# The first feed-forward product on four row strips of the array instead of one full pass

## The chip, the cores and the metric

The kernel runs on one core of one Trainium2 chip. A core has a matrix engine (TensorE, PE in the profile, with its weight loads listed as PEld), a vector engine (DVE), a scalar engine (ACT), GpSimd (POOL) and a queue that issues DMAs (SP). The metric is the device time of one launch in microseconds (us). Before the change the median is 1633.15 us, of two runs at 1631.74 and 1634.57.

## The reference

An induced-attention layer over four batches of 12480 rows with 128 channels, then a feed-forward layer with squared ReLU and 2048 units, all in float32:

```python
def mab(q, kv):
    s = scale * (q @ kv.transpose(0, 2, 1))
    s = s - s.max(-1, keepdims=True)
    a = np.exp(s)
    a /= a.sum(-1, keepdims=True) + 1e-09
    return a @ kv
h = mab(I, x)                       # 32 inducing rows attend to x
attn = mab(x, h)                    # x attends to the 32 rows
y = np.maximum(attn @ w_in, 0.0)
out = y * y @ w_out
```

The second attention gives `attn = a @ h` with only 32 weights a row, so `attn @ w_in = a @ (h @ w_in)`: the kernel forms `h @ w_in` (32 rows x 2048 units) once a batch, and the first feed-forward product contracts over 32 rows, not over 128 channels.

## The kernel before, in words

**Units.** Each batch is cut into 13 units of 960 rows, a unit into two blocks of 480 rows. For each unit `First` does the attention of the 32 inducing rows (scores, exponentials, a mix into a running sum). When a batch is through, `first_end` closes it: it makes `hT` (channels x 32 rows) and then `hw`, the product `h @ w_in`, in four tiles `hw0` to `hw3` of 512 units each (`wide`, `part`, `rest` inside it, lines 612 to 627). `Second` does the other attention for a unit: its scores go into a narrow PSUM tile `na`, and nine DVE steps and one ACT step (`weigh`) turn them into weights `sw`, which are written to DRAM (`far`, line 716) and read back in another layout (`st`, line 721).

**Precision.** Products that matter run in the type float32r, whose operands are rounded. Each value is therefore split in a rounded part ("hi") and the rest ("lo"). In `hw` before the change, rows 0 to 63 hold the hi part and rows 64 to 127 the lo part; in `st` the 128 rows hold hi and lo of the 32 weights twice. So a single product over 128 rows adds up all four combinations, hi and lo of `hw` with hi and lo of `st`. `pairs` (line 232) spreads the 32 columns of `hT` over 128 places for that.

**Feed-forward.** `ffn_block` works on one block of 480 rows, in four quads of 512 units: 416 quads in all. A quad takes

- `wide` (line 802): four products `h<-st,hw`, two into each of two PSUM buffers of the pool `ps_h`, which has just two buffers of two banks; each pair of products is a task of its own and takes one buffer;
- `relu` (line 810) on ACT, one for each buffer, then `square` (line 820) on ACT over the whole quad;
- `high` (line 827 on DVE, or line 825 as a casting DMA issued by POOL, about every second quad) and `low` (line 831) on DVE, which split the squares in hi and lo;
- twelve products into `op` (line 847): hi with `wo_hi`, hi with `wo_lo`, lo with `wo_hi`.

At the end of a block DVE transposes `op` into `rows` (line 863) and SP stores it.

**Order.** Nothing is scheduled at run time. Every step is a `Task` with an engine, an assumed duration, a due time, its needs and the buffers that it takes, and `Plan.run` lists the tasks in the order of a simulated run by these numbers; each engine then executes its own tasks strictly in that order. A task has a `mode` when it uses the matrix engine in tiles: `"n"` marks narrow products with 32 output partitions each, on four column strips of the array (`na`, `nb`). Where two tasks on PE differ in mode, the plan adds `SWITCH`, 95 ns. The attention of later units (`narrow`) is slipped in between the quads of the current unit.

Of the kernel before, what the change touches and what calls it, by code (L numbers as in the profile page):

```python
# [20 lines left out]
P = 128  # L21
# [144 lines left out]
def induced_attention_then_squared_relu_ffn(  # L166
# [24 lines left out]
    W_AHEAD = 9000.0  # L191
    LAG, CAST_LAG, TWICE = 1500.0, 1500.0, (4, 8)
# [16 lines left out]
    plan = Plan(dict(xn=3, early=EB, xt=NU + 2, m=2, h=2, o=2, g=GB, hi=HB, lo=LB, st=2, sw=1, rows=1, xq=2, hw0=1, hw1=1, hw2=1, hw3=1, words=3, set=2), T_MAIN)  # L209
# [22 lines left out]
    pairs = const.tile([P, 2, M, 2], F32, name="pairs")  # L232
    for k in range(Q):
        nc.vector.tensor_copy(pairs[:, k // 2, :, k % 2], same_m[:, 0, :])

# [325 lines left out]
    def first_end(b, due, step, wide_due, wide_step):  # L561
# [36 lines left out]
        def spread():  # L598
            v["join"] = att.tile([P, P], F32, tag="join", name=f"join_{b}", bufs=1)
            nc.vector.tensor_scalar(  # L600
                v["join"], pairs.rearrange("p j m a -> p (j m a)"), v["wq"], v["rz"], ALU.mult, ALU.mult
            )

        def join():
            v["hp"] = bank(f"htp_{b}")
            nc.tensor.matmul(v["hp"][:C, :P], last.acc, v["join"], start=True, stop=True)

        def joined():
            s["hT"] = att.tile([C, P], F32, tag="hT", name=f"hT_{b}")
            copy(tj, s["hT"], v["hp"][:C, :P])  # L610

        def wide(k):
            if b:
                v["wp", k] = bank(f"wp_{b}_{k}")
            elif k < 2:
                v["wp", k] = ps_h.tile([P, 2, 512], F32, tag="h", name=f"wp_{b}_{k}")[:, 0, :]
            else:
                v["wp", k] = ps_o.tile([P, 512], F32, tag="o", name=f"wp_{b}_{k}")
            nc.tensor.matmul(v["wp", k], s["hT"], w_in_sb[:, k * 512:(k + 1) * 512], start=True, stop=True)  # L619

        def part(k):
            s["hw", k] = hw_pool.tile([P, 512], F32R, tag=f"hw{k}", name=f"hw_{b}_{k}")
            nc.scalar.copy(s["hw", k], v["wp", k])

        def rest(k):
            lo = slice(2 * M, 4 * M)
            nc.vector.tensor_sub(s["hw", k][lo], v["wp", k][lo, :], s["hw", k][lo])
# [14 lines left out]
        for k in range(F // 512):  # L642
            bw = Buffer("m" if b else "h" if k < 2 else "o")
            s["bhw", k] = Buffer(f"hw{k}")
            d = wide_due + k * wide_step
            t = add("PE", 870, lambda k=k: wide(k), d, [s["joined"], w_ins[k]], takes=[bw, s["bhw", k]])
            p = add("ACT", 650, lambda k=k: part(k), d, [t], reads=[bw, s["bhw", k]])
            s["wide"].append(add("DVE", 725, lambda k=k: rest(k), d, [p], reads=[bw, s["bhw", k]]))


    class Second:
# [6 lines left out]
        def score(self, where):  # L658
            for q in range(Q):
                for to, from_, n in LANES[q]:  # L660
                    nc.tensor.matmul(  # L661
                        where[q * M:(q + 1) * M, to:to + n], self.s["hT"][:, :2 * M].rearrange("c (m a) -> c m a", a=2)[:, :, 0],
                        self.s["xt"][self.u][:, from_:from_ + n], start=True, stop=True,
                    )

        def weigh(self, scored, where, bank_, due, step):
# [51 lines left out]
            def back_in():  # L718
                s["st", u] = att.tile([P, 2, BLK], F32R, tag="st", name=f"st_{n}")
                for j in range(2):  # L720
                    nc.sync.dma_start(
                        s["st", u][2 * j * M:2 * (j + 1) * M].rearrange("r k (i n) -> r (k i) n", i=2).bitcast(F32),
                        v["far"].rearrange("(q m) a n -> (m a) q n", q=Q),
# [227 lines left out]
```

## Time and profile before

| | before |
|---|---|
| median of the runs | 1633.15 us |
| the profiled execution's own time | 1636.69 us |
| its span, first to last instruction | 1634.9 us |
| PE / PEld busy | 98% / 81% |
| ACT / DVE / POOL busy | 94% / 89% / 8% |
| mean granted TensorE clock | 0.989 |

The page of the profile lists for every engine how long it was busy, then groups of equal instructions (count, total busy time, mean length of one, idle time of the engine before them and who ended it). The chain of waits goes back from the last instruction to what released it, and so on to the start. Matrix products are pipelined: a row's mean is the time from its issue to its modelled end, not the distance to the next, which is read from the starts in the timeline or from the chain.

### The profile page before, as it was taken

The page shows a single profiled execution, that of the slowest core. Times are in us where ns is not written, and L with a number is a line of the kernel's source. Part 1 is how long each engine was busy: PE and PEld are TensorE (multiplying, and loading weights), DVE is VectorE, ACT ScalarE, POOL GpSimd, SP SyncE. Part 2 cuts the span into 40 slices and gives each one's busy share as a digit, 9 for nine tenths or more (in the row PEclk, how much of TensorE's full clock was granted, in tenths as well). Part 3 has the DMA queues.
Part 4 walks back from the last instruction along what each step waited for, and adds up shares of the span by engine and source line. Part 5 has one row for each costly group of instructions (what it writes and reads, how often), then busy time and mean ns, then how long its engine had stood idle before and what let it go on. Part 6 is the DMA issues. An engine that isn't in the chain of part 4 may idle for free.

```text
span 1634.9 us, 23534 instructions
## 1 busy us (share of the span) xinstructions
PE 1596.4 (98%) x8689; PEld 1325.2 (81%) x8689; DVE 1461.1 (89%) x1598; ACT 1542.2 (94%) x1566; POOL 124.0 (8%) x218
## 2 busy tenths in 40 slices
PE   7499999999999999999999999999999999999998
PEld 4278788888888888888887888888888888888887
DVE  5799989988999989999889999999888998989897
ACT  6399999999999999999998999999999999999996
POOL 1300000000000000000000000000000000000000
PEclk9699999999999999999999999999999999999999
DMA  9389988888777888788878878766555655565653
GB/s 230 71 123 202 217 217 199 212 211 210 188 207 199 209 211 203 211 207 210 217 182 202 209 207 203 211 190 190 164 181 160 190 184 172 181 199 169 192 172 95
DMA packets 474014, 311.00 MB, mean 190 GB/s; under 512 B 365212, under 2 KB 444668, under 8 KB 473900
## 3 DMA queue, kind: packets, MB, share of 16 engines
q1 hardware_dynamic: 445100, 112.89, 38.9%
q0 software_dynamic: 28800, 196.62, 33.9%
q8 instruction: 68, 1.11, 0.3%
q14 instruction: 46, 0.38, 0.1%
HBM read 74.50 MB, written 38.34 MB: 69 GB/s over the span
## 4 chain that ended last, share of the span: by engine, by line
PE 90%; DMA 3%; ACT 3%; DVE 2%; issue 1%; SPq 1%; DVEq 0%; ACTq 0%
PE op L847 63%; PE h L802 21%; PE na L661 2%; DMA xn<-in_x_dram 1%; ACT g L810 1%; ACT g L820 1%; PE wp L619 1%; PE na L457 1%; PE nb L508 1%; DVE lo L831 1%; DMA xq<-in_x_dram 1%; PE xtp L439 1%; PE ep L488 1%; DMA far<-sw 0%; PE sp L457 0%
## 5 line engine op out<-in xcount | busy, mean ns | idle before, releaser
L831 DVE TENSOR_TENSOR lo<-g,hi 128x1920 fp32r<-128x1920 f32 x416 | 883.6, 2145 | 28.5 <-PE op L847 23.1
L810 ACT ACTIVATE g<-h 128x960 f32<-128x960 f32 x832 | 781.2, 987 | 37.2 <-PE h L802 30.4
L820 ACT ACTIVATE g<-g 128x1920 f32<-128x1920 f32 x416 | 760.9, 1829 | 4.4
L802 PE MATMUL h<-st,hw 128*128 128x480 f32 x1664 | 504.6, 387 | 16.7 <-DMA st<-far 15.8
L847 PE MATMUL op<-hi,wo_lo 128*128 128x480 f32 x1664 | 472.0, 381 | 0.0
L847 PE MATMUL op<-hi,wo_hi 128*128 128x480 f32 x1664 | 442.3, 381 | 0.0
L847 PE MATMUL op<-lo,wo_hi 128*128 128x480 f32 x1664 | 435.0, 381 | 2.6 <-DVE lo L831 2.6
L802 PEld LDWEIGHTS h<-st,hw 128*128 128x128 f32 x1664 | 306.1, 189 | 78.6 <-DVE sw L710 15.8
L847 PEld LDWEIGHTS op<-lo,wo_hi 128*128 128x128 f32 x1664 | 309.9, 188 | 54.5 <-DVE lo L831 5.8
L847 PEld LDWEIGHTS op<-hi,wo_lo 128*128 128x128 f32 x1664 | 312.1, 188 | 50.9 <-issue 2.1
L847 PEld LDWEIGHTS op<-hi,wo_hi 128*128 128x128 f32 x1664 | 310.9, 188 | 49.8 <-issue 1.6
L827 DVE CAST hi<-g 128x1920 fp32r<-128x1920 f32 x216 | 248.4, 1152 | 37.5 <-PE op L847 26.6
L825 POOL DMA_DIRECT2D hi<-g x200 | 107.0, 535 | 1424.9 <-ACT g L810 279.3
L863 DVE STREAM_TRANSPOSE rows<-op 128x480 f32<-128x480 f32 x104 | 70.4, 677 | 51.2 <-PE op L847 49.5
L424 DVE STREAM_TRANSPOSE xt<-xq 128x960 f32<-128x960 f32 x39 | 45.6, 1170 | 8.6 <-DMA xq<-in_x_dram 6.0
L661 PEld LDWEIGHTS na<-xt,hT 128*32 128x32 f32 x520 | 19.9, 110 | 25.2 <-issue 19.4
L661 PE MATMUL na<-xt,hT 128*32 128x256 f32 (+2 forms) x520 | 34.9, 351 | 0.0
L685 ACT ACTIVATE d<-d 128x256 f32<-128x256 f32 x52 | 22.8, 439 | 7.0 <-DVE d L682 7.0
L689 DVE TENSOR_REDUCE z<-d 128x8 f32<-128x256 f32 x52 | 20.7, 398 | 8.4 <-ACT d L685 8.4
L508 PE MATMUL nb<-xn,et 120*32 120x128 f32 x624 | 25.7, 275 | 0.0
L457 PE MATMUL na<-xt,indT 128*32 128x240 f32 x312 | 24.8, 373 | 0.0
L703 DVE STREAM_TRANSPOSE a<-d 128x256 f32<-128x256 f32 x52 | 23.0, 443 | 1.3
(86 smaller groups left out, 529.6 us busy)
## 6 DMA issues: line engine op xcount, KB each, us to landing
hi<-g POOLq DMA_DIRECT2D x200, 960.0 KB, 4.5
xn<-in_x_dram SPq DMA_DIRECT2D x52, 480.0 KB, 6.3
st<-far SPq DMA_DIRECT2D x104, 240.0 KB, 4.3
out_dram<-rows SPq DMA_DIRECT2D x416, 60.0 KB, 3.5
xq<-in_x_dram SPq DMA_DIRECT2D x156, 120.0 KB, 5.3
far<-sw SPq DMA_DIRECT2D x52, 240.0 KB, 2.5
words_i<-in_moe_w_in_dram SPq DMA_DIRECT2D x4, 512.0 KB, 15.8
words_o<-in_moe_w_out_dram SPq DMA_DIRECT2D x4, 512.0 KB, 7.1
```

The lines of the kernel that those rows point to most:

```text
L424: nc.vector.transpose(self.xt, v["xq"].rearrange("p g c -> p (g c)"))
L457: nc.tensor.matmul(to, indT, from_, start=True, stop=True)
L508: nc.tensor.matmul(where[q * M:(q + 1) * M, :], self.et[:, k, q * M:(q + 1) * M], self.xn[:, 2 * q + k, :], start=(k == 0), stop=(k == 1),)
L661: nc.tensor.matmul(where[q * M:(q + 1) * M, to:to + n], self.s["hT"][:, :2 * M].rearrange("c (m a) -> c m a", a=2)[:, :, 0], self.s["xt"][ ...
L802: nc.tensor.matmul(c["hp"][:, l, :BLK], s["hw", j][:, f % 4 * P:(f % 4 + 1) * P], s["st", u][:, k, :], start=True, stop=True,)
L810: nc.scalar.activation(v["g"][:, 2 * i:2 * i + 2, :], c["hp"][:, :, :BLK], AF.Relu)
L820: nc.scalar.activation(v["g"], v["g"], AF.Square)
L825: nc.gpsimd.dma_start(v["hi"], v["g"])
L827: nc.vector.tensor_copy(v["hi"], v["g"])
L831: nc.vector.tensor_sub(v["lo"], v["g"], v["hi"])
L847: nc.tensor.matmul(w["op"][:, :BLK], wo[:, 4 * j + l, :], v[name][:, l, :], start=len(done) == 1, stop=len(done) == 3 * NF,)
L863: nc.vector.transpose(w["rows"].rearrange("p g c -> p (g c)"), w["op"][:, :BLK])
```

## The change

The first feed-forward product uses the matrix engine as four row strips of 32 rows. Strip `l` holds one tile of 128 units of the quad and multiplies it by the 32 weights, so `st` holds the 32 weights four times over (once in each strip), with hi and lo side by side. A quad is now one PE task of twelve products of 32 rows, three rounds over the four strips: hi with hi, lo with hi, hi with lo; lo with lo is no longer formed. Every strip adds up in its own PSUM bank, so the task takes both `ps_h` buffers at once, and both ReLUs wait for it. The task has a mode of its own, `"r"`.

With this, `hw` is made by four narrow products for each quad (mode `"n"`) into a tile of 128 x 128, `hT` shrinks to 32 columns and `pairs` goes. `st` is read back for each block apart, by four DMAs of 120 KB for each block (before: two of 240 KB for a whole unit), with three buffers of a block each; the second block's read is due 9 us after the first's (`BACK`). The narrow task of the first unit is due 1.5 us earlier.

In PE's order in the second batch, before the change: pairs of products `h` (a block's `h_0_0_4` is the fifth pair of unit 0, block 0) stand between products `op` of the quads before.

```order
L847 MATMUL op_12_1_8574<-hi_12_1_1_8521,wo_lo 128x480 x2
L802 MATMUL h_0_0_4_8639<-st_0_8424,hw_2_8543 128x480 x2
L847 MATMUL op_12_1_8574<-hi_12_1_1_8521,wo_lo 128x480 x2
L847 MATMUL op_12_1_8574<-lo_12_1_1_8577,wo_hi 128x480 x4
L802 MATMUL h_0_0_5_8674<-st_0_8424,hw_2_8543 128x480 x2
L847 MATMUL op_12_1_8574<-hi_12_1_2_8563,wo_hi 128x480 x2
```

The same kind of place in the changed kernel, unit 1 of a later batch: the six rows of `h` are the three rounds, each over the two buffers with two strips in each.

```order
L843 MATMUL op_1_0_10999<-hi_1_0_0_10951,wo_lo 128x480 x4
L843 MATMUL op_1_0_10999<-lo_1_0_0_10979,wo_hi 128x480 x4
L798 MATMUL h_1_0_6_11043<-st_1_0_10500,hw_3_10514 128x480 x2
L798 MATMUL h_1_0_7_11044<-st_1_0_10500,hw_3_10514 128x480 x2
L798 MATMUL h_1_0_6_11043<-st_1_0_10500,hw_3_10514 128x480 x2
L798 MATMUL h_1_0_7_11044<-st_1_0_10500,hw_3_10514 128x480 x2
L798 MATMUL h_1_0_6_11043<-st_1_0_10500,hw_3_10514 128x480 x2
L798 MATMUL h_1_0_7_11044<-st_1_0_10500,hw_3_10514 128x480 x2
L843 MATMUL op_0_1_10813<-hi_0_1_3_10913,wo_hi 128x480 x4
L843 MATMUL op_0_1_10813<-hi_0_1_3_10913,wo_lo 128x480 x4
```

Two separate pairs of products have become one block of twelve that stands between two runs of `op`; the product on the far side is again one over 128 rows. Over the whole program, neighbours on PE that differ in the strips they use (all 128 x 128, narrow column strips, row strips) number 152 in the order before and 954 after.

At a change of batch, before, one product over 128 rows makes 512 units of `hw` (`wp`):

```order
L847 MATMUL op_12_0_4603<-hi_12_0_1_4593,wo_lo 128x480 x2
L619 MATMUL wp_1_4681<-w_in_sb,hT_4419 128x512
L802 MATMUL h_12_1_4_4686<-st_12_4301,hw_2_878 128x480 x2
L847 MATMUL op_12_0_4603<-hi_12_0_1_4593,wo_lo 128x480 x2
L847 MATMUL op_12_0_4603<-lo_12_0_1_4673,wo_hi 128x480 x4
```

And after, four products with 32 output partitions make the same 512 units:

```order
L843 MATMUL op_12_0_5518<-hi_12_0_1_5549,wo_lo 128x480 x2
L611 MATMUL wp_1_5676<-w_in_sb,hT_4919 32x128 x4
L843 MATMUL op_12_0_5518<-lo_12_0_1_5646,wo_hi 128x480 x4
L843 MATMUL op_12_0_5518<-hi_12_0_2_5604,wo_lo 128x480 x2
L843 MATMUL op_12_0_5518<-lo_12_0_2_5629,wo_hi 128x480 x4
```

The step keeps its place; it is shorter in streamed columns and differs in mode from its neighbours.

On SP, before, a unit's `st` follows its `far` at once:

```order
L716 DMA far_11_3997<-sw_11_3979 256x1x240
L721 DMA st_11_4006<-far_11_3997 64x4x240 x2
L867 DMA out_dram<-rows_9_1_4037 32x15x32 x4
L400 DMA xn_2_4114<-in_x_dram 120x8x128
L420 DMA xq_3_4146<-in_x_dram 32x30x32 x4
```

After, it is read in two pieces, one for each block, with stores and loads in between:

```order
L709 DMA far_10_4215<-sw_10_4182 256x1x240
L397 DMA xn_1_4260<-in_x_dram 120x8x128
L714 DMA st_10_0_4314<-far_10_4215 32x4x240 x4
L417 DMA xq_2_4336<-in_x_dram 32x30x32 x4
L863 DMA out_dram<-rows_8_0_4341 32x15x32 x4
L709 DMA far_11_4499<-sw_11_4477 256x1x240
L714 DMA st_10_1_4506<-far_10_4215 32x4x240 x4
```

SP issues eight DMAs for a unit's `st` where it issued two, and twice the bytes.

The diff:

```diff
--- before.py
+++ after.py
@@ -189,6 +189,7 @@
     PERIOD, START, T_MAIN, NARROW, STEP = 31000.0, 2500.0, 56000.0, -6000.0, 1700.0
     W_DUE = [12000.0 + 7500.0 * k for k in range(4)] + [40000.0 + 4000.0 * k for k in range(4)]
     W_AHEAD = 9000.0
+    BACK = 9000.0
     LAG, CAST_LAG, TWICE = 1500.0, 1500.0, (4, 8)
 
     ST = "ACT|DVE"
@@ -206,7 +207,7 @@
     ps_o = ctx.enter_context(tc.tile_pool(name="ps_o", bufs=2, space=PSUM))
     ps_m = ctx.enter_context(tc.tile_pool(name="ps_m", bufs=2, space=PSUM))
     far = ctx.enter_context(tc.tile_pool(name="far", bufs=2, space=bass.MemoryType.DRAM))
-    plan = Plan(dict(xn=3, early=EB, xt=NU + 2, m=2, h=2, o=2, g=GB, hi=HB, lo=LB, st=2, sw=1, rows=1, xq=2, hw0=1, hw1=1, hw2=1, hw3=1, words=3, set=2), T_MAIN)
+    plan = Plan(dict(xn=3, early=EB, xt=NU + 2, m=2, h=2, o=2, g=GB, hi=HB, lo=LB, st=3, sw=1, rows=1, xq=2, hw0=1, hw1=1, hw2=1, hw3=1, words=3, set=2), T_MAIN)
 
     def bank(name):
         return ps_m.tile([P, 512], F32, tag="m", name=name)
@@ -229,10 +230,6 @@
         nc.vector.tensor_copy(same_m[:, k, :], same_m[:, 0, :])
 
     same = same_m.rearrange("p k m -> p (k m)")
-    pairs = const.tile([P, 2, M, 2], F32, name="pairs")
-    for k in range(Q):
-        nc.vector.tensor_copy(pairs[:, k // 2, :, k % 2], same_m[:, 0, :])
-
     lane_q = const.tile([P, Q], F32, name="lane_q")
     nc.vector.tensor_reduce(
         lane_q, ident.rearrange("p (q m) -> p q m", q=Q), axis=AX.X, op=ALU.add
@@ -596,35 +593,31 @@
             nc.vector.reciprocal(v["rz"], v["rz"])
 
         def spread():
-            v["join"] = att.tile([P, P], F32, tag="join", name=f"join_{b}", bufs=1)
-            nc.vector.tensor_scalar(
-                v["join"], pairs.rearrange("p j m a -> p (j m a)"), v["wq"], v["rz"], ALU.mult, ALU.mult
-            )
+            v["join"] = att.tile([P, M], F32, tag="join", name=f"join_{b}", bufs=1)
+            nc.vector.tensor_scalar(v["join"], same_m[:, 0, :], v["wq"], v["rz"], ALU.mult, ALU.mult)
 
         def join():
             v["hp"] = bank(f"htp_{b}")
-            nc.tensor.matmul(v["hp"][:C, :P], last.acc, v["join"], start=True, stop=True)
+            nc.tensor.matmul(v["hp"][:C, :M], last.acc, v["join"], start=True, stop=True)
 
         def joined():
-            s["hT"] = att.tile([C, P], F32, tag="hT", name=f"hT_{b}")
-            copy(tj, s["hT"], v["hp"][:C, :P])
-
-        def wide(k):
-            if b:
-                v["wp", k] = bank(f"wp_{b}_{k}")
-            elif k < 2:
-                v["wp", k] = ps_h.tile([P, 2, 512], F32, tag="h", name=f"wp_{b}_{k}")[:, 0, :]
-            else:
-                v["wp", k] = ps_o.tile([P, 512], F32, tag="o", name=f"wp_{b}_{k}")
-            nc.tensor.matmul(v["wp", k], s["hT"], w_in_sb[:, k * 512:(k + 1) * 512], start=True, stop=True)
-
-        def part(k):
-            s["hw", k] = hw_pool.tile([P, 512], F32R, tag=f"hw{k}", name=f"hw_{b}_{k}")
-            nc.scalar.copy(s["hw", k], v["wp", k])
-
-        def rest(k):
-            lo = slice(2 * M, 4 * M)
-            nc.vector.tensor_sub(s["hw", k][lo], v["wp", k][lo, :], s["hw", k][lo])
+            s["hT"] = att.tile([C, M], F32, tag="hT", name=f"hT_{b}")
+            copy(tj, s["hT"], v["hp"][:C, :M])
+
+        def wide(j):
+            v["wp", j] = bank(f"wp_{b}_{j}")[:, :P]
+            for k in range(Q):
+                f = Q * j + k
+                nc.tensor.matmul(
+                    v["wp", j][k * M:(k + 1) * M, :], s["hT"], w_in_sb[:, f * P:(f + 1) * P], start=True, stop=True
+                )
+
+        def part(j):
+            s["hw", j] = hw_pool.tile([P, 2, P], F32R, tag=f"hw{j}", name=f"hw_{b}_{j}")
+            nc.scalar.copy(s["hw", j][:, 0, :], v["wp", j])
+
+        def rest(j):
+            nc.vector.tensor_sub(s["hw", j][:, 1, :], v["wp", j], s["hw", j][:, 0, :])
 
         bl, bz, bj = Buffer("m"), Buffer("m"), Buffer("m")
         t = add("DVE", 70, lanes, due, [last.shifted])
@@ -639,13 +632,13 @@
         t = add("PE", 140, join, due + step, [t, last.summed], takes=[bj])
         tj = s["joined"] = add("ACT|DVE", (200, 200), joined, due + step, [t], reads=[bj])
         s["wide"] = []
-        for k in range(F // 512):
-            bw = Buffer("m" if b else "h" if k < 2 else "o")
-            s["bhw", k] = Buffer(f"hw{k}")
-            d = wide_due + k * wide_step
-            t = add("PE", 870, lambda k=k: wide(k), d, [s["joined"], w_ins[k]], takes=[bw, s["bhw", k]])
-            p = add("ACT", 650, lambda k=k: part(k), d, [t], reads=[bw, s["bhw", k]])
-            s["wide"].append(add("DVE", 725, lambda k=k: rest(k), d, [p], reads=[bw, s["bhw", k]]))
+        for j in range(NQ):
+            bw, bh = Buffer("m"), Buffer(f"hw{j}")
+            s["bhw", j] = bh
+            d = wide_due + j * wide_step
+            t = add("PE", 350, lambda j=j: wide(j), d, [s["joined"], w_ins[j]], mode="n", takes=[bw, bh])
+            p = add("ACT", 250, lambda j=j: part(j), d, [t], reads=[bw, bh])
+            s["wide"].append(add("DVE", 220, lambda j=j: rest(j), d, [p], reads=[bw, bh]))
 
 
     class Second:
@@ -659,7 +652,7 @@
             for q in range(Q):
                 for to, from_, n in LANES[q]:
                     nc.tensor.matmul(
-                        where[q * M:(q + 1) * M, to:to + n], self.s["hT"][:, :2 * M].rearrange("c (m a) -> c m a", a=2)[:, :, 0],
+                        where[q * M:(q + 1) * M, to:to + n], self.s["hT"],
                         self.s["xt"][self.u][:, from_:from_ + n], start=True, stop=True,
                     )
 
@@ -715,16 +708,16 @@
                 v["far"] = far.tile([P, 2, LANE], F32, tag="far", name=f"far_{n}")
                 nc.sync.dma_start(v["far"], v["sw"][:, :, :LANE].bitcast(F32))
 
-            def back_in():
-                s["st", u] = att.tile([P, 2, BLK], F32R, tag="st", name=f"st_{n}")
-                for j in range(2):
+            def back_in(k):
+                s["st", u, k] = att.tile([P, 2, BLK], F32R, tag="st", name=f"st_{n}_{k}", bufs=3)
+                for r in range(Q):
                     nc.sync.dma_start(
-                        s["st", u][2 * j * M:2 * (j + 1) * M].rearrange("r k (i n) -> r (k i) n", i=2).bitcast(F32),
-                        v["far"].rearrange("(q m) a n -> (m a) q n", q=Q),
+                        s["st", u, k][r * M:(r + 1) * M].rearrange("m a (q n) -> m a q n", q=2).bitcast(F32),
+                        v["far"][2 * k * M:2 * (k + 1) * M].rearrange("(q m) a n -> m a q n", q=2),
                     )
 
             bw = Buffer("sw")
-            self.bst = Buffer("st")
+            self.bst = [Buffer("st"), Buffer("st")]
             d = due
             t = add("DVE", 335, turn, d, [scored], reads=[bank_])
             t = add("DVE", 320, top, d + step, [t])
@@ -738,8 +731,11 @@
             th = add("DVE", 210, high, d + 5 * step, [t], port=True, takes=[bw])
             tl = self.split = add("DVE", 340, low, d + 5 * step, [th], port=True, reads=[bw])
             t = add("SP", 600, away, d + 6 * step, [tl], reads=[bw], moves=900)
-            t = add("SP", 1100, back_in, d + 7 * step, [t], takes=[self.bst], moves=1900, lag=LAG if due > T_MAIN else 0.0)
-            self.ready = [t, t]
+            self.ready = [
+                add("SP", 2300, lambda k=k: back_in(k), d + 7 * step + k * BACK, [t], takes=[self.bst[k]], moves=1950,
+                    lag=LAG if due > T_MAIN else 0.0)
+                for k in range(2)
+            ]
 
 
     def narrow(second, f, g, due, step, before=None):
@@ -790,31 +786,31 @@
             v = {}
             due = t0 + j * part
             bg, bhi, blo = Buffer("g"), Buffer("hi"), Buffer("lo")
+            bh = [Buffer("h"), Buffer("h")]
+            c = {}
+
+            def wide():
+                for i in range(2):
+                    c[i] = ps_h.tile([P, 2, 512], F32, tag="h", name=f"h_{n}_{2 * j + i}")
+                for m, (x, y) in enumerate(((0, 0), (1, 0), (0, 1))):
+                    for l in range(Q):
+                        r = slice(l * M, (l + 1) * M)
+                        nc.tensor.matmul(
+                            c[l // 2][:, l % 2, :BLK], s["hw", j][r, x, :], s["st", u, k][r, y, :],
+                            start=m == 0, stop=m == 2,
+                        )
+
+            t = add("PE", 600, wide, due, [second.ready[k], s["wide"][j]], mode="r", takes=bh,
+                    reads=[second.bst[k], s["bhw", j]], late=LATE_G1)
             relus = []
             for i in range(2):
-                bh = Buffer("h")
-                c = {}
-
-                def wide(l, i=i, c=c):
-                    if l == 0:
-                        c["hp"] = ps_h.tile([P, 2, 512], F32, tag="h", name=f"h_{n}_{2 * j + i}")
-                    f = 4 * j + 2 * i + l
-                    nc.tensor.matmul(
-                        c["hp"][:, l, :BLK], s["hw", j][:, f % 4 * P:(f % 4 + 1) * P], s["st", u][:, k, :],
-                        start=True, stop=True,
-                    )
-
-                def relu(i=i, c=c):
+                def relu(i=i):
                     if i == 0:
                         v["g"] = pools["g"].tile([P, 4, BLK], F32, tag="g", name=f"g_{n}_{j}", bufs=GB)
-                    nc.scalar.activation(v["g"][:, 2 * i:2 * i + 2, :], c["hp"][:, :, :BLK], AF.Relu)
-
-                d = due + i * part / 2
-                need = [second.ready[k], s["wide"][j]]
-                t = add("PE", 219, lambda wide=wide: wide(0), d, need, takes=[bh], reads=[second.bst, s["bhw", j]], late=LATE_G1)
-                t = add("PE", 219, lambda wide=wide: wide(1), d, [t], reads=[bh, second.bst, s["bhw", j]])
-                relus.append(add("ACT", 864, relu, d + 1000, [t] + opened[:1] + relus, late=0,
-                                 takes=[bg] if i == 0 else [], reads=[bh] + ([bg] if i else [])))
+                    nc.scalar.activation(v["g"][:, 2 * i:2 * i + 2, :], c[i][:, :, :BLK], AF.Relu)
+
+                relus.append(add("ACT", 864, relu, due + i * part / 2 + 1000, [t] + opened[:1] + relus, late=0,
+                                 takes=[bg] if i == 0 else [], reads=[bh[i]] + ([bg] if i else [])))
 
             def square():
                 nc.scalar.activation(v["g"], v["g"], AF.Square)
@@ -883,7 +879,7 @@
     first_end(0, t_end, 1000, t_end + 2000, 1000)
     t_main = T_MAIN
     seconds = {0: Second(0, 0)}
-    narrow(seconds[0], None, None, t_end + 2000, 800)
+    narrow(seconds[0], None, None, t_end + 500, 800)
     seconds[1] = Second(0, 1)
     narrow(seconds[1], None, None, t_end + 10000, 1700, seconds[0].split)
     opened = [add("POOL", 1, open_g, t_main - 2000, [firsts[NU - 1].summed])]
```

## The prediction

> **What bounds the kernel now.** I first read the page of the profiled execution: the busy shares of the engines and the chain of waits by engine.
>
> ```profile
> span 1634.9 us, 23534 instructions
> PE 1596.4 (98%) x8689; PEld 1325.2 (81%) x8689; DVE 1461.1 (89%) x1598; ACT 1542.2 (94%) x1566; POOL 124.0 (8%) x218
> PE 90%; DMA 3%; ACT 3%; DVE 2%; issue 1%; SPq 1%; DVEq 0%; ACTq 0%
> ```
>
> PE leads the chain with 90% of the span, but ACT is close behind. A share over the whole span mixes the start with the steady part, so I then asked for windows (columns: length, busy time of PE, PEld, DVE, ACT and POOL, granted clock, DMA share, GB/s).
>
> ```profile
> 60.00:100.00 40.00, 23.36 (x119) 15.99 (x118) 32.80 (x46) 23.87 (x28) 6.79 (x5) 0.70 0.76 110
> 100.00:400.00 300.00, 298.12 (x1681) 248.67 (x1680) 276.97 (x306) 292.35 (x299) 19.43 (x36) 1.00 0.84 201
> 700.00:1000.00 300.00, 299.22 (x1636) 249.19 (x1629) 274.28 (x299) 289.97 (x294) 21.89 (x40) 1.00 0.81 200
> ```
>
> These are not the same in kind: PE's busy time is pipelined and nearly fills any window, so it says little by itself; ACT's 290 to 292 of 300 us says that ACT could run only 2.5 to 3.4% faster than now. What PE really needs is the distance between products, read from the chain in a stretch without attention work (start, length, what).
>
> ```profile
> 839.43 3.48 PE op L847 x16
> 842.91 0.44 PE h L802 x2
> 844.66 0.86 PE wp L619 x2
> ```
>
> Sixteen products of 480 columns take 3.48 us, 0.2175 us each; a pair of `h` takes the same 0.44. A quad has 4 + 12 products, so 3.48 us; 416 quads make 1448 us of a steady part of some 1540 us (the first `h` starts at 77 us). Narrow products, transposes and `wp` fill most of the rest. PE is the bound: what the change adds to PE per quad is added 416 times. ACT's own need for a quad comes from its timeline.
>
> ```profile
> 802.84 1.84 ACT L810 ACTIVATE g<-h 128x960 f32<-128x960 f32 x2
> 804.54 1.84 ACT L820 ACTIVATE g<-g 128x1920 f32<-128x1920 f32 x1
> 806.24 1.86 ACT L810 ACTIVATE g<-h 128x960 f32<-128x960 f32 x2
> ```
>
> Two ReLUs from 802.84 to 804.54 and a square to 806.24: 1.70 each, 3.40 us for a quad, against PE's 3.48.
>
> **The change, part by part.**
>
> *The products themselves.* Removed: 4 x 0.2175 = 0.87 us a quad. Added: three rounds over four strips. If the strips of a round run at once, a round takes what one product takes, 0.2175 us, since each strip still streams 480 columns: 0.65 us. The saving is 0.2175 x 416 = 90 us. The trace has no row strips, but it has column strips, in the narrow products.
>
> ```profile
> 821.76 1.02 PE L847 MATMUL op<-lo,wo_hi 128*128 128x480 f32 x4
> 822.72 0.63 PE L661 MATMUL na<-xt,hT 128*32 128x256 f32 x9
> 822.72 0.16 PEld L661 LDWEIGHTS na<-xt,hT 128*32 128x32 f32 x8 [0.33 <-issue]
> 824.17 0.71 PE L802 MATMUL h<-st,hw 128*128 128x480 f32 x2
> 824.72 0.82 PE L847 MATMUL op<-hi,wo_hi 128*128 128x480 f32 x3
> 823.35 0.45 PE na L457 x6
> 823.80 0.44 PE nb L508 x16
> 824.24 0.64 PE h L802 x2
> ```
>
> (The first five rows are of the timeline, the last three of the chain.) Eight weight loads of about 0.11 us each are through in 0.16 us, so they start some 7 ns apart and overlap: strips do work side by side. I carry the 7 ns over as a stagger of 0.02 us a phase, 8 us in all.
>
> *Switching between full pass and strips.* This is the term that decides. The four `op` products start at 821.76 and stand 0.2175 apart, so the last starts at 822.41; the first narrow load starts at 822.72. That is 0.31 us where 0.2175 is usual: 0.09 us until the array is empty. Normally the next load lies under the running product; after a switch it does not, and the load's own time shows. On the way back two `h` products take 0.55 us to the next `op` (824.17 to 824.72) instead of 0.435, so 0.11 us for an exposed load of 128 columns; the chain gives the whole way back as 0.64 - 0.44 = 0.20 us. The strips' loads have 128 columns as well, so I take 0.20 for each direction. That this is no single case shows in the waits: PE's load queue stood idle for no visible cause ahead of narrow products 54 times, 0.36 us on average.
>
> ```profile
> PEld na L661 <- issue: 19.4, 54, 1.5
> ```
>
> The order has 954 neighbours of unequal mode instead of 152, so 802 more switches (blocks of strips that stand next to narrow products share one): 802 x 0.20 = 160 us. From below, the price is 0.09, where the load is hidden after all (72 us); from above 0.22, with a slower start of four strips (176 us). Whether the row strips switch like the column strips is not shown in any row. [...]
>
> *`hw` by narrow products.* Before, `wp` takes 0.86 us for 512 units (chain row above), sixteen times. After, four products of 128 columns, half of the eight of `nb` that take 0.44: 0.22. Their switches are in the 802 already. 16 x 0.64 = 10 us saved, of which three batches, 8 us, lie on the bound path. The casts that make `hw` on ACT and DVE get smaller too; they lie beside PE, and I cost them at nothing.
>
> *The start.* The first `h` waits for `st`, and the DVE steps that lead there are held up by `hw`:
>
> ```profile
> PE h L802 <- DMA st<-far: 15.8, 1, 15.8
> 57.75 0.45 DVE L675 STREAM_TRANSPOSE d<-na 128x256 f32<-128x256 f32 x1
> 59.97 0.69 DVE L627 TENSOR_TENSOR hw<-wp,hw 64x512 fp32r<-64x512 f32 x1 [1.31 <-ACT hw L623]
> 68.53 1.48 DVE L710 TENSOR_TENSOR sw<-a,sw 128x256 fp32r<-128x256 f32 x1
> 72.59 1.27 SPq L721 DMA_DIRECT2D st<-far x2
> ```
>
> Between the first DVE step at 57.75 and the end of the last at 70.01 lie three `hw` steps of 0.69 and waits for `wp` such as the 1.31, some 3.4 us together; most of that goes, and the narrow products now come ahead of the first `wp`. Two more DMA issues (1.27 us for two) take 1.3 back, and the weights of the second product, prepared on the same DVE, are not ready much sooner. I take 3 us off, with bounds of 0 and 5.
>
> *Reading `st` twice.* 960 instead of 480 KB a unit:
>
> ```profile
> st<-far SPq DMA_DIRECT2D x104, 240.0 KB, 4.3
> q1 hardware_dynamic: 445100, 112.89, 38.9%
> ```
>
> That adds 25 MB to 113 on this queue, between 2% (at its mean price per packet) and 9% (at its price per byte) of the 16 DMA engines, on top of the 0.81 to 0.84 of the windows. SP issues six more DMAs a unit, 3.8 us of 31. If SP waits for a free `st` buffer, the stores and `xq` loads behind it wait too. `st` is read a unit ahead and PE waited for it only at the start, so I cost this at nothing; without the cover up to 10 us.
>
> *One task for both buffers.* The twelve products wait until both ReLUs of the quad before are done, 1.70 us after they start. PE has twelve `op` products in between, 2.61 us, so the wait is covered, except at places with eight or fewer: 34 in the order, each at most 0.5 us or so, up to 15 us. PE already waits for ReLUs, so I add nothing:
>
> ```profile
> PEld h L802 <- ACT g L810: 10.8, 38, 1.3
> ```
>
> **Sum.** -90 + 8 + 160 - 8 - 3 = +67 us on a span of 1634.9, so 1702 and 1704 of own time (1.8 us lie outside the span). The median of the runs stands 3.5 us under the profiled execution's 1636.69: 1700 us, 4% slower.
>
> **The rivals.**
>
> 1. *Cheap switches.* The balance turns at (90 + 8 + 3 - 8) / 802 = 0.116 us a switch. For it: a strip has a quarter of the rows, so it may empty sooner, and a load may slip in early. Against it: both 0.09 and 0.11 are the same at every narrow group. At 0.09 to 0.12 a switch the time is 1612 to 1636, no change that can be told; chance 0.15. If row strips need no switch at all, PE falls by some 90 us and ACT becomes the bound: it is idle 8 to 10 of 300 us, so at most 3%, 1590, and 1610 with half of that lost in the tighter coupling of PE and ACT; chance 0.13.
>
> 2. *The strips do not overlap in full.* Slower by much more. If loads of 128 columns in different row strips queue one behind the other, a phase is 12 x 0.11 = 1.32 us instead of 0.67: 270 us more, 1970. [...] The trace speaks against queueing for column strips only. [...] Chance 0.12 for the two together.
>
> 3. The forecast itself, 1666 to 1725 (switches of 0.16 to 0.20, and up to 25 us of waits for buffers and DMAs): chance 0.60.
>
> **How the numbers follow.** The likeliest case gives 1700. The range leaves out rival 2 (0.12) and the free switch (about half of 0.13): 1615 to 1735. About 2% either way is what a measurement of this kernel can tell from no change, 1600 and 1666. Faster by more: 0.04, the best part of the free switch. Within: 0.15 for the cheap switch, 0.09 for the rest of the free one, 0.02 from the lower edge of the forecast: 0.26. Slower by more: 0.58 and 0.12: 0.70.
>
> **What would show it.** In the changed profile, the chain of a steady stretch should have about 1.05 us from the start of a block of twelve `h` to the first `op` behind it, PE's loads ahead of each `h` block and each `op` block behind it should stand idle 0.2 to 0.35 us with no visible cause, and ACT should fall to about 93% in the windows where it is at 97 now. Rounds some 0.22 us apart would confirm the overlap; rounds of 0.4 the queueing. The forecast is wrong if blocks take under 0.87 us with both switches, or if PE waits for ReLUs or for `st` at each quad.

## The result, and the profile after

The changed kernel takes 1715.72 us (1713.66 and 1717.78 in two runs) where the kernel before took 1633.15: a ratio of 1.0496, with a 95% interval from 1.0472 to 1.052. It is slower by 5%. The forecast was 1700, with a range of 1615 to 1735 and a chance of 0.70 on slower by over 2%.

The page of the changed kernel's profile, the same parts that were shown of before: span, busy shares, the chain of waits by engine.

```profile
span 1716.0 us, 30832 instructions
PE 1665.6 (97%) x12113; PEld 1198.3 (70%) x12113; DVE 1458.6 (85%) x1595; ACT 1576.2 (92%) x1565; POOL 123.6 (7%) x218
...
PE 85%; DMA 5%; DVE 3%; ACT 3%; SPq 2%; issue 1%; DVEq 0%; ACTq 0%
```

PE still leads the chain, but its share went from 90% to 85%, and DMA, DVE and SP's queue took more. The windows say where (columns as in the prediction):

```profile
100.00:400.00 300.00, 288.49 (x2142) 208.35 (x2133) 256.43 (x289) 273.05 (x273) 18.49 (x34) 0.98 0.89 204
400.00:700.00 300.00, 298.84 (x2197) 215.23 (x2199) 263.21 (x287) 285.16 (x283) 20.16 (x38) 1.00 0.87 213
700.00:1000.00 300.00, 292.81 (x2166) 210.15 (x2162) 251.46 (x278) 275.15 (x273) 19.53 (x37) 0.99 0.84 208
1300.00:1600.00 300.00, 300.00 (x2056) 217.59 (x2053) 256.87 (x245) 290.25 (x255) 21.12 (x40) 1.00 0.62 190
```

ACT fell from 292 to 273 us in the first of these, so it is now held back. PE, which nearly filled its windows before, has holes of 12 us in all in the first and 7 in the third, and none in the last, where the DMA share is the lowest of these four (0.62). The DMA share alone doesn't tell where they are: the second window has 0.87 and a hole of just 1 us.

A steady stretch of PE's timeline shows the phase itself (start, length, what), with the weight loads below it:

```profile
840.08 1.03 PE L843 MATMUL op<-hi,wo_hi 128*128 128x480 f32 x4
841.04 0.93 PE L798 MATMUL h<-st,hw 32*128 32x480 f32 x12
841.90 1.13 PE L843 MATMUL op<-lo,wo_hi 128*128 128x480 f32 x4
842.86 1.02 PE L843 MATMUL op<-hi,wo_lo 128*128 128x480 f32 x4
...
841.04 0.52 PEld L798 LDWEIGHTS h<-st,hw 32*128 32x128 f32 x12 [0.33 <-issue]
841.90 0.73 PEld L843 LDWEIGHTS op<-lo,wo_hi 128*128 128x128 f32 x4 [0.34 <-issue]
```

The last of four `op` products starts at 840.08 + 3 x 0.2175 = 840.73, the first strip at 841.04: 0.31 us, of which 0.09 is more than usual. The next `op` is issued at 841.90 and needs until 842.86 for four products, 0.96 where 0.87 is usual. From 840.73 to 842.86 are 2.13 us; before the change the same nine full products would take 1.96. The phase costs 0.17 us more than it replaces. Inside it, the three rounds start at 841.04, 841.37 and 841.58, and the four strips of a round within 0.015 us of each other: after a first step of 0.325, which shows the exposed load of 0.11, the distance is 0.21. Of 416 phases, 332 have such a wait of PE's loads ahead of the strips and 350 behind them with no visible cause:

```profile
PEld h L798 <- issue: 116.3, 332, 8.3
PEld op L843 <- issue: 116.0, 350, 0.6
DVE rows L859 <- DMA out_dram<-rows: 20.1, 4, 10.2
PE op L843 <- DVE lo L827: 16.7, 6, 7.9
```

The last two rows have grown. Before the change they were:

```profile
DVE rows L863 <- DMA out_dram<-rows: 1.6, 2, 1.4
PE op L847 <- DVE lo L831: 2.6, 5, 0.8
```

Now DVE waits up to 10.2 us for stores, and PE behind it up to 7.9 us. Where holes on PE are given below, they are the distance from the start of one product to the start of the next, 0.4 us more than such a wait.

The start of the n-th square on ACT, one for each quad, taken from both traces, shows when the time was lost:

| square | before, us | after, us | difference |
|---|---|---|---|
| 0 | 81.6 | 70.4 | -11.3 |
| 16 | 140.4 | 134.4 | -6.0 |
| 48 | 261.3 | 275.0 | +13.7 |
| 208 | 861.0 | 902.5 | +41.5 |
| 240 | 985.4 | 1038.4 | +53.0 |
| 415 | 1618.7 | 1701.3 | +82.6 |

From 48 to 208 the changed kernel loses 27.8 us in 160 quads, from 240 to 415 it loses 29.6 in 175: 0.17 us a quad both times, the cost of a phase. Between 16 and 48 and between 208 and 240 it loses 19.7 and 11.5 where 0.17 a quad would make 5.4 each: about 20 us of stalls. The start gives back 11 in these two traces. That number is good to some 2 us only: in the four kernels below that keep the changed kernel's start the first square comes between 71.7 and 72.6 us, and in the kernel before with a second `rows` buffer at 79.5.

### The profile page after: what moved, and what is told of

Same layout as the page of the kernel before. It is cut to its first block, busy times and chain, and to the rows that moved or that the text cites. A ratio compares the mean times of both kernels' runs of the same rounds, so it can differ in the third digit from the quotient of the medians.

```text
span 1716.0 us, 30832 instructions
## 1 busy us (share of the span) xinstructions
PE 1665.6 (97%) x12113; PEld 1198.3 (70%) x12113; DVE 1458.6 (85%) x1595; ACT 1576.2 (92%) x1565; POOL 123.6 (7%) x218
## 4 chain that ended last, share of the span: by engine, by line
PE 85%; DMA 5%; DVE 3%; ACT 3%; SPq 2%; issue 1%; DVEq 0%; ACTq 0%
PE op L843 62%; PE h L798 19%; PE na L654 2%; DMA xn<-in_x_dram 2%; DMA hi<-g 2%; ACT g L810 1%; DVE lo L827 1%; SPq L417 1%; PE na L454 1%; PE nb L505 1%; ACT g L816 1%; DMA far<-sw 1%; DMA xq<-in_x_dram 1%; DMA out_dram<-rows 1%; SPq L863 0%
## 5 line engine op out<-in xcount | busy, mean ns | idle before, releaser
L810 ACT ACTIVATE g<-h 128x960 f32<-128x960 f32 x832 | 770.5, 968 | 76.3 <-PE h L798 71.2
L816 ACT ACTIVATE g<-g 128x1920 f32<-128x1920 f32 x416 | 753.2, 1811 | 11.5
L843 PE MATMUL op<-hi,wo_hi 128*128 128x480 f32 x1664 | 466.9, 397 | 2.5 <-DMA hi<-g 1.1
L843 PE MATMUL op<-hi,wo_lo 128*128 128x480 f32 x1664 | 444.5, 384 | 0.0
L798 PE MATMUL h<-st,hw 32*128 32x480 f32 x4992 | 400.7, 414 | 11.9 <-DMA st<-far 8.4
L843 PEld LDWEIGHTS op<-hi,wo_hi 128*128 128x128 f32 x1664 | 291.0, 188 | 120.4 <-issue 65.8
L843 PEld LDWEIGHTS op<-hi,wo_lo 128*128 128x128 f32 x1664 | 304.9, 188 | 73.5 <-issue 32.4
L798 PEld LDWEIGHTS h<-st,hw 32*128 32x128 f32 x4992 | 213.8, 184 | 158.6 <-issue 116.3
L247 ACT COPY et<-ep 120x256 f32<-120x256 f32 x52 | 19.4, 373 | 7.4 <-PE ep L485 7.3
L668 DVE STREAM_TRANSPOSE d<-na 128x256 f32<-128x256 f32 x52 | 22.9, 440 | 3.6 <-PE na L654 3.6
```

The costliest lines, as they stand in the source:

```text
L668: nc.vector.transpose(v["d"].rearrange("p g m -> p (g m)"), where())
L798: nc.tensor.matmul(c[l // 2][:, l % 2, :BLK], s["hw", j][r, x, :], s["st", u, k][r, y, :], start=m == 0, stop=m == 2,)
L810: nc.scalar.activation(v["g"][:, 2 * i:2 * i + 2, :], c[i][:, :, :BLK], AF.Relu)
L816: nc.scalar.activation(v["g"], v["g"], AF.Square)
L843: nc.tensor.matmul(w["op"][:, :BLK], wo[:, 4 * j + l, :], v[name][:, l, :], start=len(done) == 1, stop=len(done) == 3 * NF,)
```

## The experiments

**Two switches and nothing else.** In the kernel before, one tiny product on one strip between the first two `h` products of a quad:

```diff
                     f = 4 * j + 2 * i + l
+                    if i == 0 and l == 1:
+                        nc.tensor.matmul(
+                            c["hp"][:, l, BLK:BLK + 16], s["hw", j][:M, :P], s["st", u][:M, k, :16],
+                            start=True, stop=True,
+                        )
                     nc.tensor.matmul(
```

> The kernel before, with one tiny product added to each quad: 32 rows, 16 columns, on a row strip, into unused columns of the first h bank, between the first two h products (nothing else reads it). It adds two switches a quad and 7 ns of streaming, and neither more st bytes nor shared buffers. Theory (a switch into or out of a row strip empties the array, 0.09 us, and shows the load, 0.11 us): 416 x 0.40 = 166 us more, about 1800 us, and in the trace 0.3 us from the last full product to the strip and 0.3 us on the way back. Rival (the changed kernel's time comes from the strips' loads, the buffers or the DMAs, and a switch is cheap): under 1670 us.

Measured, in one run: 1797.49 us, beside 1634.31 for the kernel before on the same chip, so 163 us more. The timeline of that kernel has the two full `h` products on either side of the strip:

```profile
903.09 0.38 PE L807 MATMUL h<-st,hw 128*128 128x480 f32 x1
903.40 0.27 PE L803 MATMUL h<-st,hw 32*128 32x16 f32 x1
903.60 0.49 PE L807 MATMUL h<-st,hw 128*128 128x480 f32 x1
903.93 0.59 PE L852 MATMUL op<-hi,wo_lo 128*128 128x480 f32 x2
```

From 903.09 to 903.93 two full products take 0.84 us instead of 0.435: 0.40 for a strip product of 16 columns. 0.31 us pass until the strip starts, 0.20 until the next full product, 0.33 until the one after. The price of 0.40 us for the way there and back, which the prediction split evenly, stands without any of the change's other parts.

**One task for both buffers.** The kernel before, with its four full products in one task:

```diff
-                t = add("PE", 219, lambda wide=wide: wide(0), d, need, takes=[bh], ...)
-                t = add("PE", 219, lambda wide=wide: wide(1), d, [t], ...)
...
+            t = add("PE", 876, wide, due, [second.ready[k], s["wide"][j]], takes=bh,
+                    reads=[second.bst, s["bhw", j]], late=LATE_G1)
```

> The kernel before, with the four full h products of a quad as one task that takes both h buffers, so that both ReLUs wait for all four and the next quad's products for both ReLUs; no strips. Theory (this coupling is covered by the twelve op products in between): 1633 to 1648 us. Rival (the coupling is a main part of what the change costs): 1670 us or more.

Measured: 1638.93 us, ratio 1.0028 (1.0019 to 1.0038): 4.6 us. PE is covered, as said. What the coupling does change is on ACT, in this kernel's timeline:

```profile
1404.75 1.83 ACT L812 ACTIVATE g<-h 128x960 f32<-128x960 f32 x2
1406.62 1.81 ACT L818 ACTIVATE g<-g 128x1920 f32<-128x1920 f32 x1
1408.33 1.81 ACT L812 ACTIVATE g<-h 128x960 f32<-128x960 f32 x2
1410.17 1.81 ACT L818 ACTIVATE g<-g 128x1920 f32<-128x1920 f32 x1
```

Quad follows quad at 3.55 us (1406.62 to 1410.17), where the rows of before in the prediction had 3.40. The order now puts a quad's square right behind its own second ReLU, and it starts 1.84 to 1.87 us after the first ReLU, when both are finished, instead of 1.70. In the kernel before, a ReLU of the next quad stands between at 250 of the 416 squares; here, and in the changed kernel, at none.

**The reads of `st` twice.** The kernel before, with each read of `st` issued again into a DRAM buffer:

```diff
+                again = far.tile([P, 2, BLK], F32, tag="again", name=f"again_{n}")
+                for j in range(2):
+                    nc.sync.dma_start(again[2 * j * M:2 * (j + 1) * M]..., v["far"]...)
...
-            t = add("SP", 1100, back_in, ...
+            t = add("SP", 2300, back_in, ...
```

> The kernel before, with every read of st issued a second time into a DRAM buffer that nobody reads: the doubled bytes and DMA issues of the changed kernel alone. Theory (the two long stalls of the changed kernel, 8.2 us and 6.4 us on PE, come from SP and the DMA engines being overloaded): 10 to 20 us more, 1643 to 1653 us, with long waits of DVE for the stores of rows. Rival (they come from the changed order): 1633 us as before, no such waits.

The bytes read are those of the changed kernel, but the kernel issues 208 DMAs for them where the changed one issues 416, it also writes 25 MB to DRAM, and the longer assumed time can move other tasks in the order.

Measured: 1646.96 us, ratio 1.0069 (1.0047 to 1.0091): 12.7 us, as expected. The place differs: the longest wait of DVE, 7.8 us, was for a load (`xq`), and the longest for a store was 4.1.

```profile
DVE xt L424 <- DMA xq<-in_x_dram: 13.9, 3, 7.8
...
154.57 13.17 SPq L420 DMA_DIRECT2D xq<-in_x_dram  x6
```

The first row is of the waits, the second of SP's timeline: six issues took SP 13.2 us, where the median of one `xq` issue in the kernel before is 0.67. DVE's wait for that load ends at 168.0 us, and PE has a hole of 7.5 us from 163.8 on, for lack of `lo`.

**Half the reads in the changed kernel.** Strips 2 and 3 multiply a tile that is read once:

```diff
+                if "held" not in state:
+                    state["held"] = const.tile([P, BLK], F32R, name="held")   # read once
-                for r in range(Q):
+                for r in range(2):
...
-                            c[l // 2][:, l % 2, :BLK], s["hw", j][r, x, :], s["st", u, k][r, y, :],
+                            ..., s["st", u, k][r, y, :] if l < 2 else state["held"][r, :],
```

> The changed kernel, with only strips 0 and 1 of st read for each block; strips 2 and 3 multiply a tile that is read once at the start (so half of the first product is wrong from the second block on). The bytes and the number of st DMAs are those of the kernel before. Theory (DMA load makes the long stalls): 10 to 20 us less than the changed kernel, 1696 to 1706 us, and no wait of DVE for the stores of rows over 2 us. Rival (the order makes them): 1716 us, the stalls stay.

The bytes are those of the kernel before; the number of `st` DMAs is 208, where the kernel before has 104.

Measured: 1711.86 us (1711.29 to 1713.27), about 4 us less than the changed kernel; 10 to 20 were expected. The long waits for the stores are gone, and with them PE's holes of 8.2 us at 188 us and of 6.4 us at 983 us:

```profile
DVE rows L866 <- DMA out_dram<-rows: 3.1, 2, 1.6
...
150.28 1.18 DVE L421 STREAM_TRANSPOSE xt<-xq 128x960 f32<-128x960 f32 x1 [7.27 <-DMA xq<-in_x_dram]
```

But one hole of 5.5 us on PE at 149 us remains, and the second row, of DVE's timeline, shows what is behind it: DVE waits 7.3 us for an `xq` load. In the trace, the two stretches that hold the stalls (squares 16 to 48 and 208 to 240) take 13.7 us less than in the changed kernel, so they lost most of their 20 us. A part of that does not arrive in the time: the first square comes 2.2 us later than in the changed kernel, and quads are slower by 0.007 us (48 to 208) and 0.021 us (240 to 415). Why the quads got slower stays open.

**A second buffer for the stores.** The changed kernel with two `rows` tiles:

```diff
-            w["rows"] = att.tile([P, BLK // M, M], F32, tag="rows", name=f"rows_{n}", bufs=1)
+            w["rows"] = att.tile([P, BLK // M, M], F32, tag="rows", name=f"rows_{n}", bufs=2)
```

> The changed kernel with two buffers for rows, so that DVE doesn't stand still while the stores of the block before are behind other DMAs. Theory (the long stalls come in by DVE waiting for that one buffer): 6 to 15 us less, 1700 to 1710 us, and no DVE wait for the stores. Rival (another late DMA stops DVE or PE in the same place): 1713 us or more.

Measured: 1704.85 us, ratio to before 1.0424 (1.0403 to 1.0445): 11 us less. DVE waits for no store any more; what is left is a PE hole of 5.1 us at 149 us, where DVE waits 6.6 us for an `xq` load, as with half the reads. The way of the long stall is visible in the changed kernel's trace, first SP, then DVE:

```profile
173.63 9.91 SPq L417 DMA_DIRECT2D xq<-in_x_dram  x4
183.64 5.84 SPq L863 DMA_DIRECT2D out_dram<-rows  x4
...
191.50 0.68 DVE L859 STREAM_TRANSPOSE rows<-op 128x480 f32<-128x480 f32 x1 [10.22 <-DMA out_dram<-rows]
```

Four `xq` issues held SP for 9.9 us, the stores behind them came late, DVE stood still 10.2 us for its one `rows` buffer, and PE had its hole of 8.2 us for lack of `lo`. Elsewhere SP did stand still for a free `st` buffer, 75 times in the changed kernel, where the longest such wait was 0.6 us before:

```profile
SPq L714 <- PE h L798: 324.0, 75, 10.5
```

None of these waits is what made the two long stalls: from 150 to 200 us there is none, and from 955 to 992 us the longest is 0.3.

**A fourth round.** The changed kernel, with lo times lo:

```diff
-                for m, (x, y) in enumerate(((0, 0), (1, 0), (0, 1))):
+                for m, (x, y) in enumerate(((0, 0), (1, 0), (0, 1), (1, 1))):
```

> The changed kernel with a fourth round in each quad (lo with lo), four more strip products, no more switches. Theory (the strips of a round run at once, so a round costs 0.2125 us, the distance of the rounds in its trace): 416 x 0.2125 = 88 us more, about 1800 us. Rival (part of the phase is loads that queue, 0.11 us each): 4 x 0.11 x 416 = 183 us more, 1895 us or more.

Measured, in one run: 1798.1 us, 82 us more than the changed kernel, or 0.20 a quad. Four more strip products cost as much as one full product (0.2175): the strips overlap, and their loads do not queue.

**One round.** The changed kernel with `((0, 0),)` in the same line.

> The changed kernel with only the first round (hi with hi) of each quad; lo with hi and hi with lo are left out, so the result is less exact. The switches stay. Theory: PE loses 416 x 0.425 = 177 us, needs 3.25 us a quad and falls behind ACT with 3.40; ACT becomes the bound and the time stops at 1595 to 1625 us, not at 1540. Rival (ACT has more room than its busy share shows): under 1580 us.

Measured, in one run: 1657.1 us. The direction holds, the floor is 32 us higher than the top of what was expected. ACT leads the chain:

```profile
ACT 41%; DVE 20%; issue 16%; PE 14%; DMA 6%; SPq 2%; DVEq 0%; POOLq 0%; ACTq 0%
...
1400.16 1.81 ACT L810 ACTIVATE g<-h 128x960 f32<-128x960 f32 x2
1402.00 1.81 ACT L816 ACTIVATE g<-g 128x1920 f32<-128x1920 f32 x1
1403.72 1.81 ACT L810 ACTIVATE g<-h 128x960 f32<-128x960 f32 x2
1405.56 1.81 ACT L816 ACTIVATE g<-g 128x1920 f32<-128x1920 f32 x1
```

3.56 us a quad (1402.00 to 1405.56), as with one task for both buffers, not the 3.40 on which the expectation stood. Even with two thirds of the strip products gone, squares 320 to 408 of this kernel are 3.575 us apart on average, where the kernel before has 3.556. The rest of the 1657 is mostly stalls: PE has holes of 7.4, 8.3 and 9.1 us at 148, 192 and 952 us, and in the stretches around them (squares 16 to 48 and 208 to 240) this kernel loses 20 and 7 us against the kernel before.

**The early narrow products, alone.** The kernel before with one due time changed:

```diff
-    narrow(seconds[0], None, None, t_end + 2000, 800)
+    narrow(seconds[0], None, None, t_end + 500, 800)
```

> The kernel before with one edit of the change alone: the first unit's narrow products are due 1.5 us earlier. Theory (most of the 11 us that the changed kernel gains at the start comes from having these products and their DVE steps ahead of the hw steps): 1622 to 1630 us. Rival (it comes from the smaller hw products and casts): 1632 us or more.

Measured: 1641.25 us, ratio 1.0033 (1.0015 to 1.0051), not the 1622 to 1630 expected. The first square does come at 76.7 instead of 81.6 us, so this edit makes up to 4.9 of the 11.3 us at the start; the rest would then come from the smaller `hw` steps, which was not tried by itself. But two holes on PE eat the gain: 3.7 us at 183, where DVE waits 3.9 us for a store, and 5.6 us at 498, where PE waits 5.2 us for `st`, which SP issued late, after 9.2 us of waiting for its `far` to land.

**The same with a second `rows` buffer**, room for it from one buffer less of two attention tiles, and the second `rows` buffer by itself:

```diff
-    narrow(seconds[0], None, None, t_end + 2000, 800)
+    narrow(seconds[0], None, None, t_end + 500, 800)
...
-            w["rows"] = att.tile(..., name=f"rows_{n}", bufs=1)
+            w["rows"] = att.tile(..., name=f"rows_{n}", bufs=2)
```

> The kernel before with the first unit's narrow products due 1.5 us earlier and with two buffers for rows (room for it from one buffer less of two small attention tiles). Theory (the early narrow products gain 5 us at the start, and their gain was lost later to DVE standing still for the stores, which a second buffer removes): 1623 to 1630 us, better than both kernels. Rival (another late DMA takes the place of the stores): 1633 us or more.

> The kernel before with only the second buffer for rows. Theory (before, DVE waited just 1.6 us for the stores): no change, 1630 to 1637 us.

Measured: 1638.26 us for both edits, ratio 1.0016 (0.9997 to 1.0035), and 1635.21 for the buffer alone, ratio 0.9997 (0.9986 to 1.0008). The buffer alone does nothing, as expected. Both together are no better than the kernel before: its runs spread from 1631 to 1648. The profiled one took 1634.55, one of the faster; it was 6.2 us ahead of the trace of the kernel before at square 48 and 2.1 us at the last, without a hole over 2 us on PE. What eats the early start there is open. Against the kernel with the buffer alone, its first square comes 1.8 us sooner (77.7 and 79.5). No version beat the kernel before.

## Why the prediction was right, and where it was off

**What bounds the kernel.** PE was the bound, and what was added to it came out in full: 163 us for two switches a quad, 82 us for a round, each in one run.

**The sum.** On the span it was +67 us, and +81 were measured. The table of squares puts 70 on the steady part, as in the sum, about 20 on stalls and 11 back at the start. So the forecast was right by its main term. Two other terms were wrong, nothing for the stalls and 3 us for the start; that they err in opposite directions, and leave the time only 16 us off, is luck.

**The products.** "A round takes what one product takes": 0.21 us between rounds, and 0.20 a quad for a fourth round. The stagger, put at 0.02 us a phase, is 0.009 to 0.014 us within a round of these rows.

**The switch.** The term that decided was 802 x 0.20 us. Its 0.20 was read from column strips; that row strips cost the same was my assumption, which no row of the kernel before shows. The runs show it: 0.09 and 0.11 us in the changed kernel's rows, 0.40 us for a switch there and back in the first experiment. Four traces agree on it. From the start of the last full product ahead of the strips to the start of the second one behind them, less 0.435 for two full products, the median is 0.40 us with one strip product of 16 columns, 0.62 with one round, 1.06 with three and 1.27 with four: 0.40 and then 0.22 for each round. The steady part of the sum, 160 - 90 + 8 - 8 = 70 us, is 0.168 us a quad; 0.17 was measured in both undisturbed stretches.

One sign that I gave was set in the wrong place: about 1.05 us from the start of a block of strips to the first `op` behind it, with a value under 0.87 against the forecast. The rows have 0.86 (841.04 to 841.90). The cost of the switches is there all the same, but 0.09 us of it lies ahead of the block's start and about 0.1 behind the start of the first `op`. With both, a phase takes about 1.05 us.

**The start.** I took 3 us off with 5 as the bound; it was 11, or some 2 less by the spread of the other kernels. The step was mis-sized: I put a number only on the `hw` steps that stood in DVE's way, and none on the narrow products that come ahead of `wp`. Alone, these bring the first square forward by 1.8 to 4.9 us in the experiments; the rest was not tried by itself.

**Reading `st` twice.** I costed this at nothing, "without the cover up to 10 us". The cover that I meant held: PE waited for `st` only at the start, 8.4 us in all, where it was 15.8 before. What failed is that I asked only whether PE waits for `st`, and put no price on the stores and loads that wait behind its reads. The stalls cost about 20 us by that way. The mechanism that I named, stores and loads held up behind other DMAs on SP, is the one that the trace shows (9.9 us for four `xq` issues and 5.8 for four stores at the first long stall, 5.2 and 5.2 at the second), though at the two long stalls SP was held by its own slow issues of `xq` and of the stores, not by a wait for an `st` buffer. About the same reads cost the kernel before 12.7 us, and a second `rows` buffer saved the changed kernel 11. Halving the bytes took 13.7 us out of the two stretches with stalls but only 4 off the time, so how much of the 20 us is bytes and how much is the changed order is not settled.

**One task for both buffers.** PE's wait was covered, as argued: 4.6 us. I had not looked at ACT's order, where the coupling costs 0.15 us a quad; it does not show in the changed kernel because PE is slower than that: squares 320 to 408 are 3.70 us apart there, against the 3.55 of the coupled order.

**The rivals.** Cheap switches fell with the first experiment (163 us for 416 switches there and back), strips that queue with the fourth round. Strips that overlap only in part, which the 0.12 on the second rival also covers, fell with the distance of 0.21 us between rounds: one full product takes 0.2175. Queueing strips were priced too low: 0.11 us is the part of a load that shows after a switch, while the load itself takes 0.18 us in the changed kernel (the mean of `LDWEIGHTS h`). The fourth round, at 0.20 us for four loads and products, excludes either price.

The price of the first rival seems too low as well: with free switches I gave 1590 to 1610 us because ACT was idle 8 to 10 of 300 us, with ACT's need at 3.40 us a quad. In the new order ACT needs 3.56. The kernel with one round gives PE about as little to do as free switches would (by an estimate from the rows, 0.62 + 12 x 0.2175 = 3.23 us a quad against 3.26), and it came to 1657. That time holds stalls, and free switches without them were not tried; but nothing here shows that they would have made the kernel faster.

## What to carry to other kernels

Before splitting full products over row strips, count the changes of mode in the program's order and price each from a row in which some other tiled product already stands: here 0.20 us, so a phase of strips between full products has to save 0.4 us, two full products of 480 columns, before it gains anything. When the bound engine is relieved, the next one's need has to be read from the order that the change makes, since a step that stands directly behind the one it depends on starts later: here a square 1.84 us after the start of its two ReLUs where it was 1.70, so a quad took ACT 3.55 us and not 3.40. A queue with time to spare (SP's issues of DMAs took 799 of 1716 us in the changed kernel) can still hold a store long enough to stop two engines, here DVE for 10.2 us and PE for 8.2, if the store's buffer is single.

## What the runs showed of the hardware that was not expected

Row strips overlap almost perfectly: twelve products of 32 rows and 480 columns start within 0.55 us, four to a round with starts at most 9 ns apart in the rows above, and a round takes 0.21 us.

A tiny product on a strip that stands alone between full products costs nearly two of them: 0.40 us for 16 columns. A whole round of four strips with 480 columns in the same place costs 0.62.

An ACT instruction that reads what the one before it writes starts after that one's end (1.84 us after the start of two ReLUs), an independent one 0.14 us sooner (1.70), before the one ahead has ended.

Issuing a DMA can hold SP: four issues of 120 KB in rows of 128 bytes took 9.9 us in a window (100 to 400 us) in which the DMA engines were 89% busy, and six took 13.2 in the kernel with the reads doubled, where the median of one such issue is 0.63 us in the changed kernel and 0.67 in the kernel before.
